# Windowed attention scores in blocks of 64 queries by 192 keys instead of strips of 32 by 160

## The chip, the cores and the metric

The program runs on one NeuronCore of a Trainium2 chip. The metric is the device time of one execution in microseconds (us). Three runs of the kernel before took 289.28, 289.46 and 292.43 us; the median is 289.46 us. The engines are PE (matrix multiply, with PEld for its weight loads), DVE (vector), ACT (scalar, does the exponentials), POOL and SP (issues most DMAs). PSUM is the memory that PE writes its results to, in banks of 512 fp32 per partition.

## The reference

Two parts are computed. The first is causal attention within a window of 128 keys, for 8 batches, 8 heads, 576 positions and a head size of 64, with a linear bias per head:

```python
scores = scale * np.matmul(q, k.transpose(0, 1, 3, 2))
rel = pos[:, None] - pos[None, :]
bias = slopes[:, None, None] * (-np.abs(rel))[None]
mask = (rel >= 0) & (rel < 128)
scores = np.where(mask, scores + bias[None], -1e9)
attn = softmax(scores); attn_out = attn @ v
```

The second is a soft mixture of experts over all 4608 tokens of 512 features: token logits against 32 slots, a softmax over the tokens that makes the slot inputs, two matrix products per expert (8 experts, 512 to 1024 to 512), and a softmax over the slots that mixes the slot outputs back.

## The kernel before, in words

**Groups.** The attention is done in 72 groups, one after another. A sequence of 576 queries is cut into four tiles of 128 queries (t = 0 to 3) and a tail of 64 (t = 4). A group is one tile and four heads (g = 0 or 1), or the tail with all eight heads: 9 groups per batch, 8 batches. In each group four slots of 128 by 128 scores are made, two per PSUM bank, and a pair of banks (`s4s`) alternates between even and odd groups. Heads of the two parities (par) lie in partitions 0 to 63 and 64 to 127, so a product over the 64 features of a head uses one half of the rows of the PE array, and the other parity the other half at the same time.

**Scores before.** For t of 1 to 4, the four strips of 32 queries go to four column ranges of the array (`64*32` in the rows: 64 array rows by 32 columns). Each strip sees its own 160 keys. L259 writes the bias as a product of ones with a ramp, eight matmuls of 320 columns in bf16; L266 adds q times k on top, sixteen matmuls of 160 columns in fp32, which the trace shows as 32 records, since an fp32 matmul is two. For t = 0 there is no earlier key: two bias matmuls of 256 columns (L247) and four score matmuls of 128 columns (L252, 8 records), all on `64*128` pieces of the array.

**The masked copy.** A query sees 128 keys, part of them in its own tile and part in the one before. `merge` folds the two onto 128 columns: `copy_predicated` overwrites one half with the other wherever a mask says so (L281, 512 columns for t of 1 to 3; L283, 256 columns for the tail). For t = 0, L279 writes a large negative number into the masked places instead.

**Order of the work.** All five engines' queues are written out by hand and run in order. Iteration i does, on DVE: `merge` of group i, row maximum (L301), reciprocal of the sums of group i-1 (L313), the exponent's bias (L304), normalising of group i-1 (L317). On ACT: the copy of the flipped probabilities of group i-3 (L379), now and then a copy of flipped attention outputs (L447) and of finished ones (L426), then four exponentials of group i (L357). POOL adds up for L313 (L309) and splits the flipped probabilities into the part for the own tile and the part for the one before (L381, L383). PE: transposes of group i-3 (L372), attention times v of group i-4 (L410), the scores of group i+1, then what the mixture needs (L438 transposes, L456 logits, L477 and L502 transposes, L514 slot sums). SP issues q, k, v and weight loads. After the 72 groups (from about 215 us) the experts and the mixing follow, which the diff does not touch.

Of the kernel before, what the change touches and what calls it, by code (L numbers as in the profile page):

```python
# [10 lines left out]
F32 = mybir.dt.float32  # L11
# [13 lines left out]
P = 128  # L25
# [9 lines left out]
KB = 32  # L35
# [21 lines left out]
def width(t):  # L57
    return P if t < 4 else TAIL

# [9 lines left out]
def tile_attn_softmoe(  # L69
# [20 lines left out]
    mask_u = cst[:, 0:P].bitcast(I32)  # L90
    mask_t = cst[:, P:P + TAIL].bitcast(I32)
# [14 lines left out]
    ramp = cpool.tile([P, 2, 2, WIN], BF16, name="ramp")  # L106
    ones = cpool.tile([P, P], BF16, name="ones")
    area = cpool.tile([P, 19, HW], F32, name="area")

    kall = kq[:, 0:NB * P].rearrange("p (n j w) -> p n j w", n=NB, j=NPAIR)  # L110
    qs = [kq[:, NB * P + 2 * P * i:NB * P + 2 * P * i + 2 * P] for i in range(3)]
# [66 lines left out]
    def load_k(b, t, eng=None):  # L178
        o, e = 4 * P * t, min(4 * P * (t + 1), NB * P)
        (eng or nc.sync).dma_start(kq[:, o:e], kd[b, :, o:e])  # L180
# [25 lines left out]
    with tc.manual_schedule(engines=ORDERED):  # L206
        warm = area[:, 2].bitcast(BF16)[:, 0:512]
        nc.vector.memset(warm, 0.0)
        nc.vector.memset(low, LOW)
        nc.vector.memset(ramp, 0.0)  # L210
        nc.vector.memset(ones, 1.0)
        nc.vector.memset(fine[:, 10:11], -1.0)
        nc.gpsimd.memset(cst[:, 0:P], 1.0)
# [12 lines left out]
        nc.gpsimd.memset(lgm, LOW)  # L226
        nc.gpsimd.memset(lne[:, :, NS:NS + 1], EPS)
        nc.gpsimd.memset(area[:, 3, 0:P], 1.0)
        nc.gpsimd.affine_select(
            unit_r, area[:, 3, 0:P], [[1, P]], ALU.is_equal, 0.0, base=0, channel_multiplier=-1)  # L230
        load_v()
        nc.scalar.dma_start(cst[:, P:], cstd)
        nc.scalar.dma_start(phi, phid)
        for t in range(2, NT):
            load_k(0, t)

    def scores(i):
        b, t, g = groups[i]
        s4 = s4s[i % 2]
        parts = [s4[:, 0:2], s4[:, 2:4]]  # L240
        if i == 0:
            parts = [ps_1.tile([P, 2, 2 * P], F32, tag="xp", name="s4_0"), pq[:, 0].rearrange("p (u w) -> p u w", u=2)]
            parts = parts[::-1]
        qt = qs[i % 3].rearrange("p (j w) -> p j w", w=width(t))
        if t == 0:
# [4 lines left out]
            for jj in range(2):  # L250
                for par, rows in enumerate(half):
                    nc.tensor.matmul(  # L252
                        parts[par][:, jj, 0:P], lhsT=qt[rows, jj], rhs=kall[rows, 0:4, 2 * g + jj],
                        start=False, stop=(jj == 1))
        else:
            strips = [(c // 2, c % 2) if t == 4 else (g, c) for c in range(4)]
            for par, rows in enumerate(half):
                for c, (h, r) in enumerate(strips):
# [3 lines left out]
            for jj in range(2):  # L262
                for par, rows in enumerate(half):
                    for c, (h, r) in enumerate(strips):
                        m0 = 4 * (t - 1) + r
                        nc.tensor.matmul(  # L266
                            s4[32 * c:32 * c + 32, 2 * par + jj, 32 * r:32 * r + WIN],
                            lhsT=qt[rows, 2 * h + jj if t == 4 else jj, 32 * r:32 * r + 32],
                            rhs=kall[rows, m0:m0 + 5, 2 * h + jj], start=False, stop=(jj == 1))
        st[groups[i]] = {"s4": s4, "parts": parts}  # L270

    ALL, LO, HI = slice(0, 4), slice(0, 2), slice(2, 4)

    def merge(key, us=ALL):
        t = key[1]
        s4 = st[key]["s4"]
        if t == 0:
            m = len(range(4)[us])
            nc.vector.copy_predicated(merged(key, us), bc(mask_u, 1, m), bc(low, 1, m).to_broadcast([P, m, P]))  # L279
        elif t < 4:  # L280
            nc.vector.copy_predicated(s4[:, :, P:2 * P], bc(mask_u, 1, 4), s4[:, :, 0:P])  # L281
        else:
            nc.vector.copy_predicated(s4[:, :, 0:TAIL], bc(mask_t, 1, 4), s4[:, :, P:P + TAIL])  # L283

    def merged_at(key):
        return P if 0 < key[1] < 4 else 0

    def merged(key, us):
        o = merged_at(key)
        if number[key] == 0:  # L290
            if isinstance(us, int):
                return st[key]["parts"][us // 2][:, us % 2, 0:P]
            return st[key]["parts"][us.start // 2][:, :, 0:P]
        return st[key]["s4"][:, us, o:o + P]

    def rowmax(key, us):
        if "mx" not in st[key]:
            o = P - merged_at(key)
            st[key]["mx"] = st[key]["s4"][:, :, o] if number[key] else work.tile([P, 4], F32, tag="mx", name="mx")
            st[key]["nb"] = work.tile([P, 4], F32, tag="nb", name="nb")  # L300
        nc.vector.tensor_reduce(st[key]["mx"][:, us], merged(key, us), axis=AX.X, op=ALU.max, negate=True)  # L301

    def bias(key, us):
        nc.vector.tensor_scalar_mul(st[key]["nb"][:, us], st[key]["mx"][:, us], SCALE)  # L304
# [46 lines left out]
    def expo(key, us=ALL):  # L351
        s = st[key]
        if "sm" not in s:
            s["p4"] = p4s[number[key] % 3]
            s["sm"] = work.tile([P, 4], F32, tag="sm", name="sm")
        for u in range(4)[us]:
            nc.scalar.activation(  # L357
                s["p4"][:, u], merged(key, u), AF.Exp,
                bias=s["nb"][:, u:u + 1], scale=SCALE, accum_out=s["sm"][:, u:u + 1],
            )  # L360

    def flip(key, us=ALL, to=None):
        s = st[key]
        if to is not None:
            s["pt"] = to.rearrange("p u (r w) -> p u r w", r=2)
            for u in range(4)[us]:
                nc.tensor.transpose(to[:, u], s["p4"][:, u], ident)
            return
        s["pt"] = pq_p.rearrange("p r (u w) -> p u r w", u=4)
        for u in range(4)[us]:  # L370
            for r, rows in enumerate(half):
                nc.tensor.transpose(s["pt"][:, u, r], s["p4"][rows, u], ident[rows, rows])  # L372

    def split(key, us=ALL):
        s, t = st[key], key[1]
        i = number[key] % 2 if number[key] < n - 1 else 2
        m = len(range(4)[us])
        pa, pp = pas[i], pps[i % 2]
        nc.scalar.copy(pa[:, us].rearrange("p u (r w) -> p u r w", r=2), s["pt"][:, us])  # L379
        if 0 < t < 4:  # L380
            nc.gpsimd.affine_select(  # L381
                pp[:, us], pa[:, us], [[0, m], [-1, P]], ALU.is_gt, 0.0, base=0, channel_multiplier=1)
            nc.gpsimd.affine_select(  # L383
                pa[:, us], pa[:, us], [[0, m], [1, P]], ALU.is_ge, 0.0, base=0, channel_multiplier=-1)
        elif t == 4:
            nc.gpsimd.affine_select(
                pp[:, us], pa[:, us], [[0, m], [0, 2], [-1, TAIL]], ALU.is_gt, 0.0, base=0, channel_multiplier=1)
            nc.gpsimd.affine_select(
                pa[:, us], pa[:, us], [[0, m], [0, 2], [1, TAIL]], ALU.is_ge, 0.0, base=0, channel_multiplier=-1)
        s.update(pd=pa, pp=pp)  # L390

    def values(key, pairs=None, to=None):
# [5 lines left out]
        pd, pp = st[key]["pd"], st[key]["pp"]  # L398
# [5 lines left out]
        for ph in parts:  # L404
            for i in inner:
                j = 2 * g + i
                for par in range(2):
# [4 lines left out]
                        rhs=src[:, 2 * par + i] if t < 4 else src[:, 2 * par + i % 2, TAIL * (i // 2):TAIL * (i // 2) + TAIL],  # L412
# [361 lines left out]
    with tc.manual_schedule(engines=ORDERED):  # L774
# [60 lines left out]
        split(gd, LO)  # L835
# [6 lines left out]
        split(gd, HI)  # L842
# [209 lines left out]
def constants():  # L1052
    slope = 2.0 ** (-8.0 * (np.arange(H, dtype=np.float64) + 1) / H)
    slopes = (slope.reshape(2, 2, 2, 1).transpose(2, 0, 1, 3) / SCALE * np.arange(WIN)).astype(BF16_NP)
    r = np.arange(P)
    cst = np.zeros((P, TAIL + NS), np.float32)
    cst[:, 0:TAIL] = np.arange(TAIL)[None, :] <= (r % TAIL)[:, None]
# [65 lines left out]
```

## Time and profile before

| | |
|---|---|
| three runs | 289.28, 289.46, 292.43 us |
| the profiled execution | 288.49 us, of which the span from the first to the last instruction is 286.0 us |
| PE busy in the span | 253.9 us (89%), 5535 matmul records |
| DVE busy | 221.6 us (77%) |
| ACT busy | 205.6 us (72%) |
| POOL busy | 112.9 us (39%) |
| DMA | 72.61 MB, mean 254 GB/s |

A busy time is a union: two records at once count once. The shares over the whole span mix two stages: the groups up to about 210 us, where PE, DVE and ACT are all busy most of the time, and the experts behind them, where PE alone works through. The chain of waits is followed back from the last instruction: each piece is the time by which it moved the end on, from the end of the piece before.

### The profile page before, as it was taken

The page shows a single profiled execution, that of the slowest core. Times are in us where ns is not written, and L with a number is a line of the kernel's source. Part 1 is how long each engine was busy: PE and PEld are TensorE (multiplying, and loading weights), DVE is VectorE, ACT ScalarE, POOL GpSimd, SP SyncE. Part 2 cuts the span into 40 slices and gives each one's busy share as a digit, 9 for nine tenths or more (in the row PEclk, how much of TensorE's full clock was granted, in tenths as well). Part 3 has the DMA queues.
Part 4 walks back from the last instruction along what each step waited for, and adds up shares of the span by engine and source line. Part 5 has one row for each costly group of instructions (what it writes and reads, how often), then busy time and mean ns, then how long its engine had stood idle before and what let it go on. Part 6 is the DMA issues. An engine that isn't in the chain of part 4 may idle for free.

```text
span 286.0 us, 13588 instructions
## 1 busy us (share of the span) xinstructions
PE 253.9 (89%) x5535; PEld 178.9 (63%) x5535; DVE 221.6 (77%) x509; ACT 205.6 (72%) x817; POOL 112.9 (39%) x218
## 2 busy tenths in 40 slices
PE   8588999799979889989979998998979899999990
PEld 4366676676757567667657765766756443687750
DVE  2889989998997999988998998798973352656451
ACT  2888889988888988998898988888783411044460
POOL 2044626662573276257527725466552011000000
PEclk9689999999999999999999999999999999999997
DMA  6645368869885987969797978866574579998997
GB/s 184 218 134 164 100 197 270 276 195 289 285 271 152 305 297 233 278 224 305 218 286 242 328 236 251 278 204 219 165 265 140 169 254 365 411 393 322 362 384 282
DMA packets 36754, 72.61 MB, mean 254 GB/s; under 512 B 4402, under 2 KB 15316, under 8 KB 36692
## 3 DMA queue, kind: packets, MB, share of 16 engines
q1 hardware_dynamic: 35972, 71.24, 75.7%
q8 instruction: 43, 0.70, 1.0%
q10 hardware_dynamic: 720, 0.51, 0.6%
q14 instruction: 19, 0.16, 0.2%
HBM read 62.29 MB, written 9.44 MB: 251 GB/s over the span
## 4 chain that ended last, share of the span: by engine, by line
PE 45%; DVE 23%; ACT 16%; POOL 7%; issue 5%; DMA 2%; DVEq 0%; ACTq 0%; POOLq 0%
ACT area L357 9%; PE xp L410 7%; DVE area L317 6%; DVE s L301 6%; PE s L266 5%; PE op L967 5%; PE hp L930 5%; PE po L992 4%; DVE s L281 3%; POOL area L381 3%; PE pq L372 3%; PE lp L456 2%; DVE s L279 2%; PE s L259 2%; ACT area L379 2%
## 5 line engine op out<-in xcount | busy, mean ns | idle before, releaser
L357 ACT ACTIVATE area<-s,nb 128x128 f32<-128x128 f32 x286 | 102.7, 391 | 13.8 <-DVE nb L304 10.4
L410 PE MATMUL xp<-area 128*64 128x128 f32 (+1 forms) x1104 | 74.5, 272 | 8.4 <-POOL area L381 5.3
L357 ACT ACTIVATION_READ_ACCUMULATOR area<-s,nb 128x1 f32 x286 | 65.4, 229 | 0.0
L410 PEld LDWEIGHTS xp<-area 128*64 128x64 f32 x1104 | 54.1, 137 | 18.0 <-POOL area L381 6.1
L317 DVE TENSOR_TENSOR area<-area,rs 128x512 f32<-128x512 f32 (+1 forms) x73 | 61.0, 836 | 1.6
L301 DVE TENSOR_REDUCE s<-s 128x4 f32<-128x512 f32 x71 | 49.5, 697 | 2.2
L379 ACT COPY area<-pq 128x512 f32<-128x512 f32 (+1 forms) x72 | 43.5, 605 | 10.7 <-PE pq L372 9.0
L266 PE MATMUL s<-kq 64*32 64x160 f32 x1792 | 43.8, 302 | 2.3 <-issue 2.3
L309 POOL TENSOR_SCALAR rs<-sm 128x4 f32<-128x4 f32 x70 | 15.0, 214 | 73.0 <-ACT area L357 71.6
L383 POOL TENSOR_SCALAR_AFFINE_SELECT area<-area 128x512 f32<-128x512 f32 x48 | 41.7, 870 | 3.3
L381 POOL TENSOR_SCALAR_AFFINE_SELECT area<-area 128x512 f32<-128x512 f32 x48 | 35.5, 740 | 15.5 <-ACT area L379 14.6
L281 DVE COPY_PREDICATED s<-cst,s 128x512 f32<-128x512 int32 x48 | 33.1, 689 | 6.1 <-PE s L266 5.6
L372 PE MATMUL pq<-unit_r,area 64*128 64x64 f32 x552 | 31.3, 233 | 3.7 <-ACT area L322 2.8
L266 PEld LDWEIGHTS s<-kq 64*32 64x32 f32 x1792 | 30.1, 107 | 4.1 <-issue 3.5
L372 PEld LDWEIGHTS pq<-unit_r,area 64*128 64x128 f32 x552 | 23.3, 140 | 11.8 <-issue 3.2
L259 PE MATMUL s<-ramp,ones 64*32 64x320 bf16 x448 | 18.7, 311 | 4.8 <-ACT area L357 4.5
L426 ACT COPY area<-xp 128x512 f32<-128x512 f32 (+1 forms) x37 | 21.4, 578 | 0.2
L447 ACT COPY area<-pq 128x512 f32<-128x512 f32 x34 | 20.7, 608 | 0.3 <-PE pq L432 0.3
L438 PEld LDWEIGHTS pq<-unit_r,area 64*128 64x128 f32 x264 | 11.1, 137 | 12.8 <-issue 9.7
L994 ACT COPY ob<-po 128x512 f32<-128x512 f32 x19 | 10.4, 591 | 11.4 <-PE po L992 11.4
L994 DVE COPY ob<-po 128x512 f32<-128x512 f32 x17 | 11.2, 686 | 6.6 <-PE po L992 6.5
L438 PE MATMUL pq<-unit_r,area 64*128 64x64 f32 x264 | 15.2, 233 | 0.9 <-ACT area L379 0.6
(173 smaller groups left out, 329.1 us busy)
## 6 DMA issues: line engine op xcount, KB each, us to landing
w<-w SPq DMA_DIRECT2D x53, 512.0 KB, 5.5
out<-ob SPq DMA_DIRECT2D x36, 256.0 KB, 3.9
kq<-q_t SPq DMA_DIRECT2D x69, 128.0 KB, 3.5
kq<-k_t SPq DMA_DIRECT2D x32, 256.0 KB, 3.9
area<-v_n SPq DMA_DIRECT2D x31, 256.0 KB, 4.2
area<-w SPq DMA_DIRECT2D x8, 512.0 KB, 4.6
area<-v_n SPq DMA_DIRECT2D x12, 128.0 KB, 4.4
kq<-w SPq DMA_DIRECT2D x3, 512.0 KB, 5.9
```

The lines of the kernel that those rows point to most:

```text
L259: nc.tensor.matmul(s4[32 * c:32 * c + 32, 2 * par:2 * par + 2, 32 * r:32 * r + WIN], lhsT=ones[rows, 0:32], rhs=ramp[rows, h], start=True, ...
L266: nc.tensor.matmul(s4[32 * c:32 * c + 32, 2 * par + jj, 32 * r:32 * r + WIN], lhsT=qt[rows, 2 * h + jj if t == 4 else jj, 32 * r:32 * r + 32],
L281: nc.vector.copy_predicated(s4[:, :, P:2 * P], bc(mask_u, 1, 4), s4[:, :, 0:P])
L301: nc.vector.tensor_reduce(st[key]["mx"][:, us], merged(key, us), axis=AX.X, op=ALU.max, negate=True)
L317: nc.vector.tensor_tensor(p4, p4, bc(rs, 2, P), op=ALU.mult)
L357: nc.scalar.activation(s["p4"][:, u], merged(key, u), AF.Exp, bias=s["nb"][:, u:u + 1], scale=SCALE, accum_out=s["sm"][:, u:u + 1],)
L372: nc.tensor.transpose(s["pt"][:, u, r], s["p4"][rows, u], ident[rows, rows])
L379: nc.scalar.copy(pa[:, us].rearrange("p u (r w) -> p u r w", r=2), s["pt"][:, us])
L381: nc.gpsimd.affine_select(pp[:, us], pa[:, us], [[0, m], [-1, P]], ALU.is_gt, 0.0, base=0, channel_multiplier=1)
L383: nc.gpsimd.affine_select(pa[:, us], pa[:, us], [[0, m], [1, P]], ALU.is_ge, 0.0, base=0, channel_multiplier=-1)
L410: nc.tensor.matmul(xp[D * par:D * par + D, j, 0:w], lhsT=v_slot[b, t - 1 + ph][:, D * h:D * h + D], rhs=src[:, 2 * par + i] if t < 4 else ...
L438: nc.tensor.transpose(xq[:, j, r], x[rows, j], ident[rows, rows])
```

## The change

`KB` goes from 32 to 64, so a block has 64 queries and a window of 128 + 64 = 192 keys. A slot no longer holds 128 queries of one head; it holds one half of the tile's queries (64) of two heads, the heads in the two partition halves. A PSUM bank then holds two slots with 2 x 192 columns.

- The bias of a bank is one matmul on a `64*128` piece with three rows that matter (two heads' ramps and, for t = 0, a row of large negative numbers), 384 columns in bf16; two matmuls per group replace eight (or the two of t = 0).
- The scores are eight matmuls on `64*64` pieces, 192 columns each (16 records), for t of 1 to 4; for t = 0 four of 64 and four of 128 columns.
- `merge` is one `copy_predicated` of 256 columns for every group, the first one in two halves.
- The layout of the slots changes in the row maximum, the transposes' destinations, POOL's patterns and the operand of attention times v; their counts and numbers of elements stay.
- The start has four small loads in place of two, and four POOL selects of 64 x 64 in place of one of 128 x 128.

On PE, the scores of a group with t > 0 and the two blocks behind them, the transposes of an earlier group and the products of a tail with v. Before (`s_0_83` is one of the two pairs of banks, `ones` the bias's weights, `pq` the transposes' bank, `xp` the bank of the products with v; of eight bias pairs the last is shown):

```order
L259 LDWEIGHTS ones
L259 MATMUL s_0_83<-ramp,ones 32x2x160
L266 MATMUL s_0_83<-kq 32x160 x16
L372 MATMUL pq<-unit_r,area 128x64 x8
L410 MATMUL xp<-area 64x64 x16
```

and with the change (the second of two bias pairs):

```order
L259 LDWEIGHTS pair_of
L259 MATMUL s_0_83<-ramp,pair_of 128x384
L267 MATMUL s_0_83<-kq 64x192 x8
L371 MATMUL pq<-unit_r,area 128x64 x8
L407 MATMUL xp<-area 64x64 x16
```

The order of the blocks is the same; the bias's product now spans all 128 columns of the array, and the scores' products, between it and the transposes, 64.

At a group with t = 0, on PE, before:

```order
L247 LDWEIGHTS ones
L247 MATMUL s_0_83<-ramp,ones 128x2x128
L247 LDWEIGHTS ones
L247 MATMUL s_0_83<-ramp,ones 128x2x128
L252 MATMUL s_0_83<-kq 128x128 x4
L372 MATMUL pq<-unit_r,area 128x64 x8
```

and with the change:

```order
L259 LDWEIGHTS pair_of
L259 MATMUL s_0_83<-ramp,pair_of 128x384
L267 MATMUL s_0_83<-kq 64x64 x4
L267 MATMUL s_0_83<-kq 64x128 x4
L371 MATMUL pq<-unit_r,area 128x64 x8
```

Here bias, scores and transposes all spanned 128 columns; now the scores between them span 64.

The diff, cut to its core:

```diff
-KB = 32
+KB = 64
...
+def slide(ap):
+    return bass.AP(ap.tensor, ap.offset, [list(ap.ap[0]), [KB, 2], [1, WIN]])
...
-        nc.gpsimd.affine_select(cst[:, 0:P], cst[:, 0:P], [[1, P]], ALU.is_gt, 0.0, base=0, channel_multiplier=-1)
+        nc.gpsimd.memset(mask, 1.0)
+        for c in range(2):
...
         for par in range(2):
-            nc.sync.dma_start(ramp[64 * par:64 * par + 1], slopes[par:par + 1])
+            nc.sync.dma_start(ramp[64 * par:64 * par + 3], slopes[par, :, 2 * P:])
+            nc.sync.dma_start(pair_of[64 * par:64 * par + 3], slopes[par, :, 0:2 * P])
...
-            for par, rows in enumerate(half):
-                nc.tensor.matmul(
-                    parts[par][:, :, 0:P], lhsT=ones[rows], rhs=ramp[rows, g, :, 0:P],
-                    start=True, stop=False)
...
-                    nc.tensor.matmul(
-                        s4[32 * c:32 * c + 32, 2 * par:2 * par + 2, 32 * r:32 * r + WIN],
-                        lhsT=ones[rows, 0:32], rhs=ramp[rows, h], start=True, stop=False)
...
-                            rhs=kall[rows, m0:m0 + 5, 2 * h + jj], start=False, stop=(jj == 1))
+        for par, rows in enumerate(half):
+            if t < 4:
+                dst, src = parts[par][:, 0:2 * WIN], slide(ramp[rows, g])
+            else:
+                dst, src = parts[par].rearrange("p (u w) -> p u w", u=2)[:, :, 0:WIN], ramp[rows, :, 0:WIN]
+            nc.tensor.matmul(dst, lhsT=pair_of[rows, int(t == 0)], rhs=src, start=True, stop=False)
+        for u in range(2):
+            h, hp = (u, g) if t < 4 else (0, u)
+            skip = max(2 * (1 - t) - h, 0)
+            m0 = 2 * (t - 1) + h
+            for par, rows in enumerate(half):
+                for jj in range(2):
+                    j = 2 * hp + jj
+                    nc.tensor.matmul(
+                        parts[par][KB * jj:KB * jj + KB, second * u + KB * skip:second * u + WIN],
+                        lhsT=qt[rows, jj if t < 4 else j, KB * h:KB * h + KB], rhs=kall[rows, m0 + skip:m0 + 3, j],
+                        start=False, stop=(u == 1))
...
-            nc.vector.copy_predicated(s4[:, :, P:2 * P], bc(mask_u, 1, 4), s4[:, :, 0:P])
...
+        x = ranges(key, us).rearrange("p a (x y) -> p a x y", y=KB)
+        m = x.shape[1]
+        if key[1] < 4:
+            to, of, keep = x[:, :, 0:6:5], x[:, :, 2:4], bc(mask.bitcast(I32), 1, m)
         else:
+            to, of, keep = x[:, :, 0:8:4], x[:, :, 2:8:4], bc(bc(mask[:, 0].bitcast(I32), 1, 2), 1, m)
+        nc.vector.copy_predicated(to, keep, of)
...
             nc.gpsimd.affine_select(
-                pp[:, us], pa[:, us], [[0, m], [-1, P]], ALU.is_gt, 0.0, base=0, channel_multiplier=1)
+                prev, own, [[-step, m], [0, 4], [-1, KB]], ALU.is_gt, 0.0, base=-i0, channel_multiplier=1)
...
-                        rhs=src[:, 2 * par + i] if t < 4 else src[:, 2 * par + i % 2, TAIL * (i // 2):TAIL * (i // 2) + TAIL],
+                        rhs=src[:, :, par, i] if t < 4 else src[:, i // 2, par, i % 2],
```

## Rows read from the trace of the kernel before

**Rows 1.** Busy time of each engine in stretches of the span: stretch, its length, then PE, PEld, DVE, ACT and POOL busy (records), granted clock, DMA share, GB/s.

```profile
8.00:16.00 8.00, 5.20 (x104) 3.63 (x104) 6.49 (x16) 6.29 (x29) 0.39 (x2) 0.58 0.65 207
...
150.00:170.00 20.00, 19.90 (x484) 15.02 (x486) 19.04 (x41) 18.00 (x78) 11.86 (x21) 1.00 0.87 278
...
16.00:209.00 193.00, 177.14 (x4462) 130.50 (x4448) 176.56 (x389) 171.08 (x717) 103.96 (x190) 1.00 0.75 236
```

**Rows 2.** The chain of waits in order of time, a stretch in which PE leads: start us, us by which the end moved on, what.

```profile
153.84 0.26 PE s L259 x8
154.10 0.54 PE s L266 x32
154.64 0.39 PE pq L372 x8
155.03 1.02 PE xp L410 x16
156.06 0.21 PE s L247 x2
156.27 0.45 PE s L252 x8
156.72 0.24 PE pq L438 x8
...
189.50 0.26 PE s L259 x8
189.76 0.54 PE s L266 x32
190.31 0.39 PE pq L438 x8
190.70 0.25 PE pq L372 x8
190.95 1.02 PE xp L410 x16
```

**Rows 3.** Groups of instructions by line, engine, operation and shape: count, busy us, mean ns of one, idle time before them and what ended it.

```profile
L281 DVE COPY_PREDICATED s<-cst,s 128x512 f32<-128x512 int32 x48 | 33.1, 689 | 6.1 <-PE s L266 5.6
...
L279 DVE COPY_PREDICATED s<-cst,fine 128x512 f32<-128x512 int32 x15 | 14.9, 997 | 0.1
...
L283 DVE COPY_PREDICATED s<-cst,s 128x256 f32<-128x256 int32 x8 | 3.4, 422 | 0.3 <-PE s L266 0.3
```

**Rows 4.** Who waited for whom between 16 and 205 us: us in total, times, longest.

```profile
PEld xp L410 <- POOL area L383: 5.4, 15, 0.6
PE xp L410 <- POOL area L381: 5.3, 6, 1.4
...
PE s L259 <- ACT area L357: 3.7, 8, 1.3
...
PE s L266 <- issue: 2.3, 4, 1.0
...
PE xp L410 <- POOL area L383: 1.3, 4, 0.4
...
PE xp L410 <- DMA area<-v_n: 0.9, 1, 0.9
```

**Rows 5.** The chain of waits in order of time, the pieces of the first scores behind the start and of the first and last masked copies on it.

```profile
11.80 0.47 PE s L259 x5
12.27 1.07 PE s L266 x24
...
15.01 0.40 PE s L259 x4
15.40 1.05 PE s L266 x25
...
16.48 0.71 DVE s L281
...
28.92 1.06 DVE s L279
...
31.99 0.62 DVE s L279
...
172.62 0.70 DVE s L281
...
205.92 1.06 DVE s L279
```

**Rows 6.** Instructions at the start in order of time: start us, us, engine (SPq is SP's DMA queue), line, operation, count, and in brackets the idle time before and what ended it.

```profile
1.56 0.59 SPq L218 DMA_DIRECT2D ramp<-slopes  x2
...
3.91 0.28 PEld L247 LDWEIGHTS <-ones 64*128 64x128 bf16 x2 [0.84 <-issue]
...
4.54 0.28 PEld L252 LDWEIGHTS pq<-kq 64*128 64x128 f32 x1 [0.34 <-DMA kq<-q_t]
```

**Rows 7.** POOL's split in two shapes by line: the pattern of 128-long runs (L383) and the tail's of 64-long runs (L388).

```profile
L383 POOL TENSOR_SCALAR_AFFINE_SELECT area<-area 128x512 f32<-128x512 f32 x48 | 41.7, 870 | 3.3
...
L388 POOL TENSOR_SCALAR_AFFINE_SELECT area<-area 128x512 f32<-128x512 f32 x7 | 5.3, 760 | 0.5
```

**Rows 8.** The chain of waits over the whole span, shares by engine, tile and line.

```profile
ACT area L357 9%; PE xp L410 7%; DVE area L317 6%; DVE s L301 6%; PE s L266 5%; PE op L967 5%; PE hp L930 5%; PE po L992 4%; DVE s L281 3%; POOL area L381 3%; PE pq L372 3%; PE lp L456 2%; DVE s L279 2%; PE s L259 2%; ACT area L379 2%
```

More of the change, by code (lines that the diff above doesn't have):

```diff
@@ L105, in tile_attn_softmoe @@
     kq = cpool.tile([P, 3 * UW], F32, name="kq")
-    ramp = cpool.tile([P, 2, 2, WIN], BF16, name="ramp")
-    ones = cpool.tile([P, P], BF16, name="ones")
+    ramp = cpool.tile([P, 2, 2 * P], BF16, name="ramp")
+    pair_of = cpool.tile([P, 2, P], BF16, name="pair_of")
     area = cpool.tile([P, 19, HW], F32, name="area")
-    kall = kq[:, 0:NB * P].rearrange("p (n j w) -> p n j w", n=NB, j=NPAIR)
-    qs = [kq[:, NB * P + 2 * P * i:NB * P + 2 * P * i + 2 * P] for i in range(3)]
+    kall = kq[:, 0:NPAIR * S].rearrange("p (n j w) -> p n j w", n=NB, j=NPAIR)
+    qs = [kq[:, NPAIR * S + 2 * P * i:NPAIR * S + 2 * P * i + 2 * P] for i in range(3)]
     half = [slice(64 * par, 64 * par + 64) for par in range(2)]
@@ L210, in tile_attn_softmoe @@
         nc.vector.memset(ramp, 0.0)
[L211 removed]
+        nc.vector.memset(pair_of, 0.0)
         nc.vector.memset(fine[:, 10:11], -1.0)
[L213 to L214 removed]
+        nc.gpsimd.memset(mask, 1.0)
+        for c in range(2):
+            rows = slice(KB * c, KB * c + KB)
+            nc.gpsimd.affine_select(
+                mask[rows, 0], mask[rows, 0], [[-1, KB]], ALU.is_ge, 0.0, base=0, channel_multiplier=1)
+            nc.gpsimd.affine_select(
+                mask[rows, 1], mask[rows, 1], [[1, KB]], ALU.is_gt, 0.0, base=0, channel_multiplier=-1)
         load_k(0, 0)
@@ L238, in scores @@
         b, t, g = groups[i]
[L239 to L240 removed]
         if i == 0:
[L242 to L243 removed]
+            parts = [pq[:, 0], ps_1.tile([P, 4 * P], F32, tag="xp", name="s4_0")]
+        else:
+            parts = [s4s[i % 2][:, 2 * par:2 * par + 2].rearrange("p u w -> p (u w)") for par in range(2)]
         qt = qs[i % 3].rearrange("p (j w) -> p j w", w=width(t))
[L245 to L269 removed]
@@ L285, in merged_at @@
-    def merged_at(key):
-        return P if 0 < key[1] < 4 else 0
-    def merged(key, us):
[L289 to L294, printed above, removed]
+        second = WIN if t < 4 else 2 * P
+        for par, rows in enumerate(half):
+            if t < 4:
+                dst, src = parts[par][:, 0:2 * WIN], slide(ramp[rows, g])
+            else:
+                dst, src = parts[par].rearrange("p (u w) -> p u w", u=2)[:, :, 0:WIN], ramp[rows, :, 0:WIN]
+            nc.tensor.matmul(dst, lhsT=pair_of[rows, int(t == 0)], rhs=src, start=True, stop=False)
@@ L296, in rowmax, with ranges @@
+    def ranges(key, us):
+        if number[key] == 0:
+            return st[key]["parts"][us.start // 2].unsqueeze(1)
+        return st[key]["s4"]
+    def merged(key, us):
+        return ranges(key, us).rearrange("p a (u w) -> p a u w", u=2)[:, :, :, 0:P]
     def rowmax(key, us):
-        if "mx" not in st[key]:
-            o = P - merged_at(key)
-            st[key]["mx"] = st[key]["s4"][:, :, o] if number[key] else work.tile([P, 4], F32, tag="mx", name="mx")
+        if "nb" not in st[key]:
@@ L371, in flip @@
             for r, rows in enumerate(half):
-                nc.tensor.transpose(s["pt"][:, u, r], s["p4"][rows, u], ident[rows, rows])
+                nc.tensor.transpose(s["pt"][:, 2 * (u % 2) + u // 2, r], s["p4"][rows, u], ident[rows, rows])
     def split(key, us=ALL):
-        s, t = st[key], key[1]
+        s, (b, t, g) = st[key], key
         i = number[key] % 2 if number[key] < n - 1 else 2
-        m = len(range(4)[us])
         pa, pp = pas[i], pps[i % 2]
         nc.scalar.copy(pa[:, us].rearrange("p u (r w) -> p u r w", r=2), s["pt"][:, us])
-        if 0 < t < 4:
+        if t:
+            own, prev = (
+                x[:, us].rearrange("p u w -> p (u w)").rearrange("p (h x w) -> p h x w", x=4, w=KB) for x in (pa, pp))
+            m, step = own.shape[1], KB if t < 4 else 0
+            i0 = step * (us.start // 2)
             nc.gpsimd.affine_select(
-                pp[:, us], pa[:, us], [[0, m], [-1, P]], ALU.is_gt, 0.0, base=0, channel_multiplier=1)
+                prev, own, [[-step, m], [0, 4], [-1, KB]], ALU.is_gt, 0.0, base=-i0, channel_multiplier=1)
             nc.gpsimd.affine_select(
[L384 to L389, printed above, removed]
+                own, own, [[step, m], [0, 4], [1, KB]], ALU.is_ge, 0.0, base=i0, channel_multiplier=-1)
         s.update(pd=pa, pp=pp)
@@ L397, in values @@
         xp = st[b, t]
-        pd, pp = st[key]["pd"], st[key]["pp"]
+        pd, pp = (st[key][x].rearrange("p (h a) (j w) -> p h a j w", a=2, j=2) for x in ("pd", "pp"))
         parts = (1,) if t == 0 else (0, 1)
@@ L834, in tile_attn_softmoe @@
         flip(gd, LO, bank("pt"))
-        split(gd, LO)
+        split(gd, EVEN)
         total(gd, HI)
@@ L841, in tile_attn_softmoe @@
         flip(gd, HI, quarters(free[2]))
-        split(gd, HI)
+        split(gd, ODD)
         token_sum(end)
@@ L1053, in constants @@
     slope = 2.0 ** (-8.0 * (np.arange(H, dtype=np.float64) + 1) / H)
-    slopes = (slope.reshape(2, 2, 2, 1).transpose(2, 0, 1, 3) / SCALE * np.arange(WIN)).astype(BF16_NP)
+    ramp = np.zeros((2, 3, 2, 2 * P))
+    ramp[:, 0:2] = slope.reshape(2, 2, 2, 1).transpose(2, 1, 0, 3) / SCALE * np.arange(2 * P)
+    ramp[:, 2, :, 0:P] = LOW
+    pair_of = np.zeros((2, 3, 2, P))
+    for jj in range(2):
+        pair_of[:, jj, :, KB * jj:KB * jj + KB] = 1.0
+    pair_of[:, 2, 1] = 1.0
+    slopes = np.concatenate([pair_of.reshape(2, 3, 2 * P), ramp.reshape(2, 3, 4 * P)], axis=2).astype(BF16_NP)
     r = np.arange(P)
     cst = np.zeros((P, TAIL + NS), np.float32)
-    cst[:, 0:TAIL] = np.arange(TAIL)[None, :] <= (r % TAIL)[:, None]
     cst[:, TAIL:] = np.arange(NS)[None, :] == (r % NS)[:, None]
```

32 lines of the change are left out of this document (14 added, 18 removed).

## The prediction, made before the changed kernel had run

> **What bounds the kernel now.** I read the busy times by stretch first, then the chain of waits, then the groups by shape, then the waits. Before the experts there are 72 groups in a row, and the stretch from 16 to 209 us holds 67 of them (2.88 us each). There the reader sees three engines side by side: PE 177.1 of 193.0 us, DVE 176.6, ACT 171.1 [rows 1]. No one engine is the bound throughout, but in the 20 us from 150 on PE has 19.90 us [rows 1], and the chain there is one PE block behind another [rows 2]. So what PE gets on top counts nearly in full in such stretches, and what DVE saves there counts for nothing.
>
> **The change part by part.** The masked copy: 48 copies of 512 columns at 689 ns and 15 with the large number at 997 ns become copies of 256 columns, for which the tail's copies give 422 ns [rows 3]. That is 48 x 0.27 + 15 x 0.575 = 21.4 us of DVE, 0.3 us per group: DVE goes from 176.6 to some 156 us in the stretch. The other DVE, ACT and POOL instructions keep their counts and sizes; POOL's new pattern has runs of 64, and the tail's row with such runs is no slower than the one with runs of 128 (760 against 870 ns) [rows 7]. I cost these at nothing; POOL is idle nearly half of the time, so a tenth more there would stay hidden.
>
> The bias on PE: eight matmuls of 320 columns moved the chain on by 0.26 us, the two of 256 columns (t = 0) by 0.21 us [rows 2]. Two of 384 columns lie between 0.26 and 0.31 us; I take 0.28.
>
> The scores on PE: for t = 0, eight records of 128 columns, two at a time, take 0.45 us, so a turn of 128 columns takes 0.11 us. Before, 32 records of 160 columns, eight at a time, take 0.54 us, four turns of 0.135 us [rows 2]. The time goes by columns and turns, not by the number of records. The new block has 16 records of 192 columns on four pieces of the array: four turns of 0.16 to 0.17 us, 0.66 us together. For t = 0 it is two turns of 64 and two of 128 columns: 0.33 us.
>
> The seam between bias and scores: before, both ran on pieces of the same shape (64 x 32, or 64 x 128 for t = 0), and the scores cost only their turns. Now the bias runs on 64 x 128 pieces and the scores on 64 x 64. What a change of the piece costs can be read: the transposes (64 x 128) behind the scores of t = 0 (also 64 x 128) add 0.24 us, behind the scores of the other groups (64 x 32) 0.39 us, and 0.25 us behind other transposes [rows 2]. So 0.14 us goes by when the column width changes although the rows of the array stay split in the same way. No row has 64 x 128 followed by 64 x 64; its bounds are 0 (the next block's start would hide it) and 0.17 us (products with v behind transposes: 1.02 us for eight turns of 0.107). I take 0.14, the row of the same kind of change. The Trainium skill ("TensorEngine Tiling (Array Packing)", Key Properties) says that a change of tiling mode, as against another tile of the same mode, drains the engine; by it the new seam costs like the others, and without it one might take 0 for a seam where only columns change. The 0.24 and 0.39 us of this trace agree with it.
>
> Sum per group with t > 0: 0.28 + 0.66 + 0.14 = 1.08 us in place of 0.26 + 0.54 = 0.80, so 0.28 more. For t = 0: 0.28 + 0.33 + 0.14 = 0.75 in place of 0.66, and the transposes behind them now also stand at a seam, 0.14 more: 0.23. In the stretch that is 54 x 0.28 + 13 x 0.23 = 18.1 us, and PE's busy time becomes 195.2 us, more than the whole stretch lasts now. PE becomes the bound everywhere.
>
> How long the stretch then gets depends on how many of PE's waits go. Not given back are the stalls that no engine causes (2.3 us in the scores' products, "issue") and the wait for v (0.9 us) [rows 4]: 195.2 + 3.2 = 198.4 us. In the other direction, some waiting is counted as busy: the weight loads for the products with v waited 5.4 us for POOL's second select where the matmuls show only 1.3 us of idle time [rows 4], so up to 4.1 us of the 195.2 can vanish. Bounds: 194.3 us (+1.3) if every wait on POOL, ACT and DVE goes, 211.1 us (+18.1) if all stay. I take 197 us, **+4.0**: the nearest row is the stretch from 150 us, where PE led and its visible waits were 0.1 us in 20 [rows 1], and of the hidden ones I give back a third.
>
> The rest: two score blocks behind the start run at a granted clock of 0.58 on the mean [rows 1] and took 0.47 + 1.07 and 0.40 + 1.05 us, all on the chain [rows 5]; by 1.08/0.80 they grow by 1.05 us. On SP's queue two more small loads go ahead of the second part of k. Two such issues took 0.59 us; the first bias stood at 3.91 us, but the first scores waited until 4.54 us for q [rows 6], so most of it is hidden: between 0 and 0.6 us, I take 0.2. The last masked copy of 1.06 us on the chain, at 205.9 us [rows 5], falls to 0.42, and PE is less full there: -0.6. Behind 209 us nothing changes. Sum: 4.0 + 1.05 + 0.2 - 0.6 = +4.65 us on the profiled execution's 288.49, 293.1 us. The median of the three runs, 289.46, is 0.97 above that execution, so **294 us**.
>
> **The rivals.**
> *The seam costs nothing, and DVE's relief carries (20%).* Then a group costs PE 0.14 us more for t > 0 and about nothing for t = 0: 7.6 us in the stretch, 184.7 us busy, below 193. For it: nothing in the trace has this very seam, and the masked copies stand on the chain with 3% (L281) and 2% (L279) of the span, 8.6 and 5.7 us, the scores' products with 5%, 14.3 us [rows 8]. Replaced along that chain, the copies give 8.6 x 0.39 + 5.7 x 0.58 = 6.6 us, and the products take 14.3 x 0.12/0.54 = 3.2 back: at most -3.4. Since ACT at 171 us and PE follow closely, I expect two thirds of it, -2.2 us, 287.3 us. It decides if the seam is under some 0.05 us, so that PE with its stalls stays at about 190 us. Against it: 0.39 against 0.24 us.
> *PE's waits stay (10%).* If POOL's splits and ACT's exponentials release PE as late as now (5.3 and 3.7 us [rows 4]), since they in turn follow PE's transposes, the 18.1 us come on top with little absorbed: +10 to +18 us, 300 to 307 us. Against it: the stretch from 150 us.
> *Fewer instructions pay (4%).* 40 records per group become 18. If each cost time of its own, PE would gain and DVE's relief would show: with ACT's 171 us as the next bound I put 282 us. Against it: 40 records in 0.80 us are 20 ns each, and they are explained by columns alone. The Trainium skill ("TensorEngine Tiling (Array Packing)", Instruction Overhead) gives some 60 cycles of overhead per matmul; by that, 22 matmuls fewer, at 2.4 GHz, would be an estimated 0.55 us per group. The trace disagrees, since 0.55 us is already two thirds of the whole 0.80.
> *The four 64 x 64 pieces don't all run at once (3%).* With two at a time the scores take 1.32 us, +44 us in the stretch, about 335 us. Against it: pieces split by rows and pieces split by columns both overlap here.
>
> **How the numbers follow.** The forecast, PE as the bound with the seam paid, gets 63%, with a range of its own from 290.5 (the lower bound) to 298.5 us. Something over 1%, 2.9 us, is what a measurement of this kernel can tell from no change: below 286.6 or above 292.4 us. Faster: 8 of the 20 points of the first rival and the 4 of the third, 12%. Within 1%: the other 12 and some 23 of the forecast's 63, 35%. Slower: 40 + 10 + 3 = 53%. The range from 286.5 to 300 leaves out about 8 points of the first rival, 4 of the third, 5 of the second and the fourth's 3.
>
> **What would show it.** In the profile after: PE busy 97% or more of the stretch and the stretch 196 to 199 us long; the seam as an end-to-end piece of 0.8 us for the 16 score records where 0.66 would be its absence; the masked copy at 422 ns; DVE falling to some 80% busy and ACT to 87%; PE's waits on POOL gone. If the piece for the scores is 0.66 us, the first rival holds; if PE waits on POOL and ACT as before, the second. The prediction is wrong if PE's busy time is not the stretch's bound, that is, if it lies below some 188 us.

## The result and the profile after

The changed kernel took 290.31 us (median of 12 runs, 289.56 to 291.12) against 289.79 us of the kernel before in the same session; the ratio is 1.0064, 95% interval [1.0039, 1.0089], some 1.9 us slower. The ratio compares fast runs alone, while the 289.79 us is a median over slower runs of the kernel before as well, so the two medians differ by 0.5 us only. In a later session, in the last experiment below, the ratio was 1.0021 [0.9984, 1.0058]. The forecast was 294 us, 1.6% slower: the time lies in the wide range of 286.5 to 300 us, a little under the 290.5 us at which the forecast's own range began, and the step is two fifths of the one forecast, or less.

The profiled execution took 290.67 us and has a span of 288.9 us. The chain of waits, shares by engine: first the kernel before, then the kernel after, and of the latter also the shares by line (L267 are the scores' products, L259 the bias, L407 the products with v, L371 and L435 the transposes):

```profile
PE 45%; DVE 23%; ACT 16%; POOL 7%; issue 5%; DMA 2%; DVEq 0%; ACTq 0%; POOLq 0%
...
PE 72%; ACT 9%; DVE 7%; POOL 5%; DMA 3%; issue 2%; DVEq 0%; ACTq 0%; SPq 0%
PE xp L407 16%; PE s L267 14%; PE pq L371 6%; PE op L964 5%; PE s L259 5%; PE hp L927 5%; ACT area L356 4%; PE po L989 3%; PE pq L435 3%; PE ap L511 3%; PE lp L453 2%; POOL area L383 2%; DVE area L314 2%; DVE s L297 2%; DMA area<-v_n 2%
```

PE has gone from 45% of the chain to 72%; the masked copies, 5% before [rows 8], are no longer in the list. The pieces of the kernel after in order of time, start us, us by which the end moved on, one group with t > 0, one with t = 0:

```profile
155.57 0.27 PE s L259 x2
155.83 0.81 PE s L267 x16
156.65 0.39 PE pq L371 x8
157.04 1.02 PE xp L407 x16
158.06 0.27 PE s L259 x2
158.33 0.50 PE s L267 x16
158.83 0.39 PE pq L435 x8
```

Against [rows 2]: bias and scores 1.08 us where 0.80 stood; for t = 0 bias, scores and the transposes behind them 1.16 us where 0.90 stood. The other blocks are as long as before. Busy time by stretch (columns as in [rows 1]):

```profile
8.00:16.00 8.00, 6.42 (x62) 3.63 (x60) 5.85 (x18) 6.16 (x29) 0.39 (x2) 1.00 0.59 195
...
16.00:209.00 193.00, 188.31 (x3358) 129.22 (x3356) 158.07 (x386) 169.86 (x714) 102.29 (x187) 1.00 0.75 236
```

In the long stretch PE rose by 11.2 us, DVE fell by 18.5, ACT hardly moved. Who waited for whom, 16 to 205 us (columns as in [rows 4]): two rows of the kernel before, then the kernel after:

```profile
ACT area L379 <- PE pq L372: 8.7, 14, 1.3
...
DVE s L281 <- PE s L266: 5.2, 7, 1.4
```

```profile
ACT area L377 <- PE pq L371: 15.0, 19, 1.6
DVE s L283 <- PE s L267: 12.9, 26, 1.4
...
PEld xp L407 <- POOL area L385: 2.6, 9, 0.3
...
PE xp L407 <- POOL area L383: 1.6, 4, 0.4
...
PE s L259 <- ACT area L356: 1.3, 2, 1.0
...
PE xp L407 <- DMA area<-v_n: 0.7, 1, 0.7
```

PE's waits on POOL and ACT shrank to about a third (5.3 to 1.6, 3.7 to 1.3 us), the weight loads' wait for POOL's second select to a half (5.4 to 2.6 us [rows 4]), and the 2.3 us without a cause inside the scores' products are gone. In their place DVE and ACT wait for PE more than before (5.2 to 12.9, 8.7 to 15.0 us). Where the time of the span came from is read off the row maxima, one per group: the fourth group's, the fifth's and the last but one's. First the kernel before, then the one after, then a second execution of the one after (experiment 8), each in order of time:

```profile
14.19 0.70 DVE L301 TENSOR_REDUCE s<-s 128x4 f32<-128x512 f32 x1
...
17.21 0.70 DVE L301 TENSOR_REDUCE s<-s 128x4 f32<-128x512 f32 x1
...
207.00 0.70 DVE L301 TENSOR_REDUCE s<-s 128x4 f32<-128x512 f32 x1
```

```profile
14.92 0.70 DVE L297 TENSOR_REDUCE s<-s 128x4 f32<-128x512 f32 x1
...
18.17 0.70 DVE L297 TENSOR_REDUCE s<-s 128x4 f32<-128x512 f32 x1
...
208.59 0.70 DVE L297 TENSOR_REDUCE s<-s 128x4 f32<-128x512 f32 x1
```

```profile
14.68 0.70 DVE L297 TENSOR_REDUCE s<-s 128x4 f32<-128x512 f32 x1
...
209.18 0.70 DVE L297 TENSOR_REDUCE s<-s 128x4 f32<-128x512 f32 x1
```

The start cost 0.73 us, and the 67 groups between took 193.67 in place of 192.81 us: 0.86 us more, though PE does about 0.27 us more in each, 18 us in all. The second execution needed 194.50 us for them, 1.69 us more, so this figure is good to about a microsecond. Behind the groups the first execution lost about another 1.3 us (the second 0.8), 0.48 of them in a stall without a shown cause, at 254.65 us among the experts' products, which the diff does not touch. Busy time in just these 67 groups (columns as in [rows 1]), before, after and the second execution:

```profile
14.19:207.00 192.81, 177.02 (x4460) 130.04 (x4458) 176.13 (x388) 170.30 (x716) 102.51 (x188) 1.00 0.76 237
```

```profile
14.92:208.59 193.67, 188.98 (x3358) 129.71 (x3356) 158.74 (x389) 170.13 (x713) 102.14 (x187) 1.00 0.75 235
```

```profile
14.68:209.18 194.50, 189.68 (x3358) 130.10 (x3356) 159.50 (x389) 170.04 (x713) 102.03 (x187) 1.00 0.75 234
```

PE's busy time rose by 12.0 us (12.7 in the second execution), and its idle time fell from 15.8 to 4.7 us (4.8).

### The profile page after: what moved, and what is told of

Same layout as the page of the kernel before. It is cut to its first block, busy times and chain, and to the rows that moved or that the text cites. A ratio compares the mean times of both kernels' runs of the same rounds, so it can differ in the third digit from the quotient of the medians.

```text
span 288.9 us, 11388 instructions
## 1 busy us (share of the span) xinstructions
PE 268.8 (93%) x4431; PEld 178.6 (62%) x4431; DVE 203.1 (70%) x509; ACT 205.7 (71%) x817; POOL 113.1 (39%) x221
## 4 chain that ended last, share of the span: by engine, by line
PE 72%; ACT 9%; DVE 7%; POOL 5%; DMA 3%; issue 2%; DVEq 0%; ACTq 0%; SPq 0%
PE xp L407 16%; PE s L267 14%; PE pq L371 6%; PE op L964 5%; PE s L259 5%; PE hp L927 5%; ACT area L356 4%; PE po L989 3%; PE pq L435 3%; PE ap L511 3%; PE lp L453 2%; POOL area L383 2%; DVE area L314 2%; DVE s L297 2%; DMA area<-v_n 2%
## 5 line engine op out<-in xcount | busy, mean ns | idle before, releaser
L407 PE MATMUL xp<-area 128*64 128x128 f32 (+1 forms) x1104 | 73.0, 271 | 2.9 <-POOL area L383 1.6
L267 PE MATMUL s<-kq 64*64 64x192 f32 (+2 forms) x1144 | 60.7, 328 | 0.0
L407 PEld LDWEIGHTS xp<-area 128*64 128x64 f32 x1104 | 53.8, 137 | 11.1 <-POOL area L385 2.6
L383 POOL TENSOR_SCALAR_AFFINE_SELECT area<-area 128x512 f32<-128x512 f32 (+1 forms) x57 | 44.3, 777 | 28.0 <-ACT area L377 26.5
L297 DVE TENSOR_REDUCE s<-s 128x4 f32<-128x512 f32 (+1 forms) x72 | 50.0, 694 | 2.2
L385 POOL TENSOR_SCALAR_AFFINE_SELECT area<-area 128x512 f32<-128x512 f32 (+1 forms) x57 | 46.3, 812 | 3.9
L267 PEld LDWEIGHTS s<-kq 64*64 64x64 f32 x1144 | 35.1, 137 | 14.3 <-issue 12.2
L283 DVE COPY_PREDICATED s<-cst,s 128x256 f32<-128x256 int32 (+1 forms) x72 | 30.4, 422 | 14.6 <-PE s L267 14.1
L371 PE MATMUL pq<-unit_r,area 64*128 64x64 f32 x552 | 31.5, 233 | 1.2 <-ACT area L319 0.8
L371 PEld LDWEIGHTS pq<-unit_r,area 64*128 64x128 f32 x552 | 23.1, 140 | 10.7 <-issue 3.3
L259 PE MATMUL s<-ramp,pair_of 64*128 64x384 bf16 x143 | 25.0, 342 | 2.1 <-ACT area L356 2.1
L310 DVE RECIPROCAL rs<-rs 128x4 f32<-128x4 f32 (+1 forms) x73 | 12.5, 172 | 9.8 <-POOL rs L306 9.2
L435 PEld LDWEIGHTS pq<-unit_r,area 64*128 64x128 f32 x264 | 10.7, 137 | 13.7 <-issue 11.9
L259 PEld LDWEIGHTS <-pair_of 64*128 64x128 bf16 x144 | 7.6, 93 | 16.2 <-issue 9.3
```

Of the source, the lines that this page charges most:

```text
L259: nc.tensor.matmul(dst, lhsT=pair_of[rows, int(t == 0)], rhs=src, start=True, stop=False)
L267: nc.tensor.matmul(parts[par][KB * jj:KB * jj + KB, second * u + KB * skip:second * u + WIN], lhsT=qt[rows, jj if t < 4 else j, KB * h:KB ...
L283: nc.vector.copy_predicated(to, keep, of)
L297: nc.vector.tensor_reduce(st[key]["mx"], merged(key, us), axis=AX.X, op=ALU.max, negate=True)
L371: nc.tensor.transpose(s["pt"][:, 2 * (u % 2) + u // 2, r], s["p4"][rows, u], ident[rows, rows])
L383: nc.gpsimd.affine_select(prev, own, [[-step, m], [0, 4], [-1, KB]], ALU.is_gt, 0.0, base=-i0, channel_multiplier=1)
```

## The experiments

Four kernels shared a chip and its runs of the kernel before (288.74 us), and four more another (289.82 us). Ratios are to the kernel before of the same session. The changed kernel itself ran beside experiments 5 to 7 only, so 1 to 4 are compared with it through ratios of different sessions.

**1. The seam taken out.** The bias of a bank in two halves of 64 columns, so that it runs on the same pieces as the scores:

```diff
-            nc.tensor.matmul(dst, lhsT=pair_of[rows, int(t == 0)], rhs=src, start=True, stop=False)
+            for jj in range(2):
+                cols = slice(KB * jj, KB * jj + KB)
+                nc.tensor.matmul(dst[cols], lhsT=pair_of[rows, int(t == 0), cols], rhs=src, start=True, stop=False)
```

> The bias of a bank is written by two matmuls on 64 x 64 pieces in place of one on a 64 x 128 piece, so bias and scores run on pieces of one shape; nothing else changes. Theory (PE is the bound of the changed kernel, and 0.14 us per group go at the seam between bias and scores): the score block's piece of the chain falls from 0.81 to about 0.66 us, PE's busy time in the groups' stretch falls by about 9 us, and, since ACT and DVE come close behind, 5 to 8 us of that reach the end: 282 to 285 us, faster than the kernel before. Rival 1 (the 0.14 us is the latency of the scores themselves and has nothing to do with the shape): the piece stays at 0.81, time within 1 us of 290.3. Rival 2 (the seam goes, but waits on POOL and ACT take its place): the piece falls to 0.66, time within 2 us of 290.3.

Measured: 284.03 us, ratio 0.9823 [0.977, 0.9876]. The chain's pieces of this kernel (L261 bias, L269 scores), a group with t > 0 and one with t = 0:

```profile
83.80 0.29 PE s L261 x4
84.08 0.65 PE s L269 x16
84.73 0.39 PE pq L437 x8
...
104.42 0.29 PE s L261 x4
104.71 0.33 PE s L269 x16
105.04 0.39 PE pq L437 x8
```

The scores' piece falls from 0.81 to 0.65 us, and the bias, with twice the matmuls, costs 0.29 in place of 0.27. So the change of the piece's width between bias and scores costs 0.16 us, and 72 groups less 0.14 us each, 10 us of PE, brought some 6 to 7 us at the end (2.0 and 2.4 points under the changed kernel's two ratios), in the theory's range. Rivals 1 and 2 fall. The chain of the whole span is now this:

```profile
PE 49%; ACT 24%; DVE 10%; POOL 8%; issue 4%; DMA 2%; DVEq 0%; ACTq 0%; SPq 0%; POOLq 0%
```

PE is back near the 45% of before, and ACT follows. The term of the expectation that missed is the busy time: PE still shows 185.15 us in the stretch from 16 to 209 us, not 9 us less, because the stretch now holds more of the program; between the same two row maxima (14.23 and 203.30 us here) it is 181.8 us, 7.2 less than in the changed kernel.

**2. DVE's saving given back to the changed kernel:**

```diff
         nc.vector.copy_predicated(to, keep, of)
+        if key[1] < 4:
+            for _ in range(1 if key[1] else 2):
+                nc.vector.copy_predicated(to[:, :, 0:1], keep[:, :, 0:1], of[:, :, 0:1])
```

> The changed kernel with the masked copy's saving given back to VectorE: one more copy of 128 columns per group (two for t = 0) that writes the same values again, about 0.29 us each, 23 us of DVE in all, a little over the 21 us that the change took off. Theory (PE is the bound, DVE at 158 of 193 us has slack): DVE rises to about 179 us, the time by 1 to 4 us, 291 to 294 us. Rival (DVE's relief is what held the loss at 0.6%, that is, PE's added time was paid for by DVE's): 8 us or more, 298 us and up.

Measured: 293.85 us, ratio 1.0176 [1.0128, 1.0225], 1.1 points over the changed kernel's 1.0064 and 1.6 over its 1.0021, 3 to 4.5 us. The rows by shape show what was given back, 23.0 us:

```profile
L283 DVE COPY_PREDICATED s<-cst,s 128x256 f32<-128x256 int32 x71 | 30.0, 423 | 6.5 <-PE s L267 6.3
L286 DVE COPY_PREDICATED s<-cst,s 128x128 f32<-128x128 int32 x78 | 23.0, 295 | 2.7
```

That is in the theory's range, and the rival is out. Without DVE's relief the change would have cost 1.8%. About four fifths of the 23 us are absorbed: PE is the bound of the changed kernel, but DVE at 158 of 193 us is not far enough off to be free, and its relief is worth something. In the 67 groups, between this kernel's row maxima (columns as in [rows 1]), PE is idle for 7.0 us where the changed kernel had 4.7:

```profile
16.12:212.01 195.89, 188.92 (x3372) 129.66 (x3368) 176.72 (x461) 170.49 (x715) 102.66 (x188) 1.00 0.73 233
```

**3. DVE's saving alone, on the kernel before:**

```diff
-            nc.vector.copy_predicated(merged(key, us), bc(mask_u, 1, m), bc(low, 1, m).to_broadcast([P, m, P]))
+            nc.vector.copy_predicated(
+                merged(key, us)[:, :, 0:64], bc(mask_u[:, 0:64], 1, m), bc(low, 1, m).to_broadcast([P, m, 64]))
...
-            nc.vector.copy_predicated(s4[:, :, P:2 * P], bc(mask_u, 1, 4), s4[:, :, 0:P])
+            nc.vector.copy_predicated(s4[:, :, P:P + 64], bc(mask_u[:, 0:64], 1, 4), s4[:, :, 0:64])
```

> The kernel before with the masked copies of t = 0 to 3 cut to 64 of the 128 columns of each slot (256 in all); this leaves out half of the masking. It is the change's relief of DVE alone, about 19 to 21 us, without any change on PE. Theory (three engines side by side, ACT at 171 and PE with its true blocks at about 172 us follow at once): 2 to 5 us faster, 285 to 288 us. Rival (DVE bounded the kernel before): 8 us or more faster, 282 us and less. Rival 2 (DVE's relief is worth nothing): within 1 us.

Measured: 285.2 us, ratio 0.9883 [0.9829, 0.9937], 3.4 us faster, in the theory's range. Less was taken off DVE than written, as the rows by shape show:

```profile
L282 DVE COPY_PREDICATED s<-cst,s 128x256 f32<-128x256 int32 x48 | 20.3, 423 | 7.0 <-PE s L266 6.5
L279 DVE COPY_PREDICATED s<-cst,fine 128x256 f32<-128x256 int32 x15 | 11.8, 788 | 0.1
```

The 48 copies halve as expected, but those that write the large number still take 788 ns, not 422. So DVE lost 15.9 us (33.1 + 14.9 [rows 3] less 20.3 + 11.8), and a fifth of it reached the end. DVE alone did not bound the kernel before.

**4. Two loads at the start in place of four,** on top of experiment 1; ramp and weights of the bias lie in one tile:

```diff
-            nc.sync.dma_start(ramp[64 * par:64 * par + 3], slopes[par, :, 2 * P:])
-            nc.sync.dma_start(pair_of[64 * par:64 * par + 3], slopes[par, :, 0:2 * P])
+            nc.sync.dma_start(lines[64 * par:64 * par + 3], slopes[par])
```

> The first run's kernel, with ramp and weights of the bias in one tile, so that two small loads at the start take the place of four. Theory (the first groups start 0.7 us late since the last of four loads lands at 4.7 us): the first bias matmul starts at about 4.2 us in place of 4.8, and the time is 0.3 to 0.7 us under the first run's. Rival (the start is hidden behind the first wait for v or for the clock): no difference to the first run, within 0.2 us.

Measured: 282.61 us, ratio 0.9799 [0.9751, 0.9847]. The first bias matmul starts at 4.45 us, where experiment 1's stood at 4.66 and the changed kernel's at 4.83 (4.59 in its second execution). In order of time, first experiment 1, then this kernel, the first bias matmuls and a later block of them:

```profile
4.66 0.53 PE L261 MATMUL pq<-ramp,pair_of 64*64 64x384 bf16 x2 [0.68 <-DMA pair_of<-slopes]
...
5.87 0.72 PE L261 MATMUL s<-ramp,pair_of 64*64 64x384 bf16 x4
```

```profile
4.45 0.46 PE L260 MATMUL pq<-lines 64*64 64x384 bf16 x2 [0.47 <-DMA lines<-slopes]
...
5.12 0.40 PE L260 MATMUL s<-lines 64*64 64x384 bf16 x4
```

The load is still what it waits for, and it came 0.2 us earlier, not the 0.6 us expected. The same block of four takes 0.40 us in this execution and 0.72 in that of experiment 1, and why is not shown. The interval overlaps that of experiment 1, so this kernel's own gain, some 0.7 us by the ratios, is not certain, nor that the loads made it. This kernel is faster than both the kernel before (by 2.0%) and the changed one.

**5. PE's added load alone, on the kernel before:**

```diff
             strips = [(c // 2, c % 2) if t == 4 else (g, c) for c in range(4)]
+            for par, rows in enumerate(half):
+                nc.tensor.matmul(
+                    parts[par][:, :, 0:WIN], lhsT=ones[rows], rhs=ramp[rows, g], start=True, stop=True)
```

> The kernel before with PE's added load alone: ahead of the eight bias matmuls of each group with t > 0 stand two more of 320 columns on 64 x 128 pieces, whose result the bias writes over, so that a group costs PE about 0.27 us more, 15 us in all; DVE keeps its full masked copies. Theory (some 5 to 7 us of what counts as busy PE before is waiting inside the blocks, besides 10 us of visible waits, and both are used up first): 4 to 8 us slower than before, and the piece of the products with v on the chain stays 1.02 us. Rival (PE's busy time is all work, as the prediction mostly took it): 10 us or more slower.

Measured: 294.65 us, ratio 1.0163 [1.0098, 1.0229], 4.7 us slower. The chain's pieces of this kernel (L258 the two added matmuls, L262 the eight of the bias):

```profile
159.16 0.24 PE s L258 x2
159.40 0.26 PE s L262 x8
159.66 0.54 PE s L269 x32
```

The added block costs 0.24 us in 56 groups, 13.4 us, and 4.7 us come out, so two thirds of PE's added work did not show in the time, although DVE kept its full copies. In the 67 groups PE's idle time fell from 15.8 to 10.5 us, which is 5.3 us of it; that the rest went into waiting that counts as busy is argued, not shown. The rival falls. The prediction's own sum misses this kernel on the other side: 177.1 + 13.4 + 3.2 - 1.4 = 192.3 us, no longer than the stretch before, because it lets every visible wait on another engine go. Here two thirds of PE's idle time stay.

**6. Both loads at once, without the change's layout** (the edits of 3 and 5 together):

> The kernel before with both loads of the change and none of its layout: masked copies cut to 256 columns (half of the masking of t = 0 to 3 is left out) and the two added bias matmuls per group with t > 0. Theory (the change is the sum of PE's 0.27 us per group and DVE's 0.3 us, nothing else): within 0.6% of the changed kernel's ratio, 0 to 3 us slower than before. Rival 1 (the prediction's size, since waits are not given back): 4.5 us or more slower. Rival 2 (the smaller number of instructions, 18 records in place of 40 per group, helped the changed kernel by itself): 3 us or more slower than the changed kernel.

Measured: 291.24 us, ratio 1.0087 [1.0052, 1.0121], 2.5 us slower than before: by 0.2 and 0.7 points above the changed kernel's two ratios. The second is a little more than the theory allowed; this kernel's DVE relief is some 4 us smaller, for the reason in 3, and its t = 0 groups are not burdened. Rival 1 falls, and by the time so does rival 2 at its price of 3 us. But the agreement in time is in part chance. Busy time of this kernel in the 67 groups, between its row maxima (columns as in [rows 1]):

```profile
13.11:209.72 196.61, 186.44 (x4561) 133.55 (x4560) 164.88 (x388) 170.73 (x715) 99.34 (x187) 1.00 0.75 233
```

Its start is 1.6 to 1.8 us shorter than the changed kernel's, and its 67 groups take 196.61 us, 2.1 to 2.9 us longer, with 10.2 us of idle PE in place of 4.7. So in the groups the two loads alone do not make up the changed kernel; that fewer instructions, or something else of the new layout, are worth some 2 us there is not excluded.

**7. No seam, but DVE's saving given back** (the edits of 1 and 2):

> The first run's kernel (bias and scores on pieces of one shape) with VectorE's saving given back as in the second run. Theory (without the seam PE and DVE are side by side again, so DVE's relief is worth as much there as in the kernel before, 3 to 5 us): 3 to 6 us slower than the first run, within 0.7% of the kernel before. Rival (with the seam gone nothing is bound by DVE): within 1.5 us of the first run.

Measured: 291.19 us, ratio 1.0075 [1.0043, 1.0107], 2.5 points above experiment 1 (of the other session), some 7 us: more than the 3 to 6 us expected, and the rival is out. With PE less full, the same 23 us on DVE cost about twice as much as in experiment 2.

**8. The changed kernel again,** next to experiments 5 to 7:

> The changed kernel once more, on the same chip as these runs. Theory: 1 to 3 us slower than before, 6 to 8 us slower than without the seam. Rival (the 0.6% was a matter of the chip): no difference to before.

Measured: 290.17 us, ratio 1.0021 [0.9984, 1.0058]. That is 0.6 us, under the 1 to 3 us expected, and alone this run could not tell it from no change, so it does not rule out the rival. With the first result the change costs 0.2 to 0.6%. Experiment 1's ratio lies 2.0 points below this one, 5.7 us, a little under the 6 to 8 us expected, and 2.4 points below the first result's.

## Why the prediction was wrong

**Right, to a few hundredths.** The masked copy of 256 columns (forecast 422 ns, measured 424). The bias of 384 columns (0.28; 0.27). The scores by turns and columns plus the seam (0.66 + 0.14 = 0.80; 0.81, and 0.65 without the seam). For t = 0 0.23 us more per group; 0.26. The seam's price was taken from transposes behind scores, another pair of shapes, and held; the Trainium skill's rule that a change of tiling mode drains the engine ("TensorEngine Tiling (Array Packing)", Key Properties) agrees with the 0.16 us of experiment 1. That PE becomes the bound: it has 72% of the chain, and taking 0.14 us per group off it gave 6 to 7 us.

**Wrong: the step from PE's added work to the length of the stretch.** The prediction added 18.1 us to a busy time of 177.1 us, kept 3.2 us of stalls, and gave back a third of the 4.1 us that it had found hidden in the busy time: +4.0 us. Measured on the row maxima it is +0.86 us, and +1.69 in the second execution. The added work was there in full, block by block, but PE's busy time in the same 67 groups rose by 12.0 us only (12.7). About 0.8 of the missing 6 us are other blocks that fall outside the two row maxima, by their counts and pieces; the other 4.6 to 5.3 us are, by this balance, waiting that had counted as busy. That is the term that was mis-sized: the prediction gave back 1.4 us of such waiting. Where it stood is not shown in full, since of the weight loads' 5.4 us only 2.8 are seen to go. The term for idle time erred the other way: 4.7 us were left where 3.2 had been kept, and they are other waits than those named, since the 2.3 us of stalls did not come back. The text named the end of the range that was nearly right, 194.3 us with every wait given back, and then chose the middle.

That so many waits could go is in part DVE's relief, which the prediction held to count for nothing where PE leads: without it PE is idle for 2.3 us more (experiment 2). It is not all of it, since experiment 6, with most of the relief, leaves 10.2 us idle. Experiment 5 adds 13.4 us of work without it, and 4.7 us come out; experiment 3 gives the relief alone, -3.4 us; experiment 2 takes it away again, 3 to 4.5 us. The sum of 5 and 3, +1.3 us, lies between the changed kernel's two results, but both together measured 2.5 us (experiment 6), and in the groups they are 2 to 3 us apart from the changed kernel, so this split is rough. It is luck, too, that the total came as near as it did: the 0.8 to 1.3 us lost behind the groups stand in no term of the forecast.

**The small terms.** The start cost 0.73 us at the fourth group, which has the first of the two slow score blocks before it, and 0.96 us at the fifth, behind both, where 0.2 + 1.05 was forecast. The two blocks grew by 0.46 and 0.17 us on the chain (their lines are in the last section, those before in [rows 5]), 0.63 us in all, and the late loads made the other 0.33 us. In the second execution the fifth group was 1.06 us late. The relief at 205.9 us (-0.6) did not come; the last groups were bound by PE as well.

**The rivals.** "The seam costs nothing" falls by the 0.81 us, "PE's waits stay" by the waits after, and four pieces at once do overlap: four turns of 0.16 us. "Fewer instructions pay" falls at its price of 282 us; a smaller gain, some 2 us in the groups, is not excluded (experiment 6). The Trainium skill ("TensorEngine Tiling (Array Packing)", Instruction Overhead) gives each matmul an overhead of some 60 cycles, and counted for every matmul that would have them pay; in experiment 1 twice the bias matmuls cost 0.02 us.

What stays open is why PE's stalls without a cause vanished. The four kernels with the layout of before (experiments 3, 5 and 6 among them) show 1.7 to 3.5 us of them in the groups, the six with the new layout none. Experiment 6, 16 to 209 us:

```profile
PE s L269 <- issue: 1.1, 3, 0.7
...
PE xp L414 <- issue: 0.8, 1, 0.8
...
PE pq L376 <- issue: 0.4, 1, 0.4
```

The profile's queue of instruction loads (q8) moved 0.57 MB with the change in place of 0.70, so the number of instructions may be behind it, but it differs together with the rest of the layout, and no run separates the two.

## What to carry to other kernels

When an engine that shares the bound gets more work, first fill its waits, and price them from the pieces of the chain (block by block, end to end) and not from a busy time, in which short waits are hidden: work added to one of three nearly full engines came out at a third (experiment 5), work taken off at a fifth (experiment 3). Once it leads nearly everywhere, a microsecond counts about two thirds (experiment 1). And what another engine saves is not free of value then, since some of these waits are on that engine (3 to 4.5 us in experiment 2). Where two blocks of matmuls with different shapes of array pieces follow each other in every round, try to give them one shape, even with twice the number of matmuls: that turned a loss of 0.6% into a gain of 1.8%.

## What the runs showed that was not expected

The granted clock in the profile of the changed kernel is 1.00 from 8 to 16 us, as the first of the two stretches above shows (0.58 before [rows 1]), but the same kind of block there takes nearly twice its later time. This kernel, in order of the chain:

```profile
12.40 0.51 PE s L259 x2
12.90 1.49 PE s L267 x16
...
16.06 0.43 PE s L259 x2
16.50 1.19 PE s L267 x16
```

against 0.27 and 0.81 us later. Its first two pieces take 1.8 to 1.9 times as long as later. In the kernel before the same blocks took 1.8 to 2.0 times as long (0.47 to 0.26 and 1.07 to 0.54 us [rows 2, 5]) at a recorded clock of 0.58 on the mean. So the durations speak for the lower of the two levels, 1.2 in place of 2.4 GHz, which the clock's record does not show here; that is an inference, and no run settles it. And a masked copy that takes its data as one number per partition, spread over 256 columns, took 788 ns on the mean where one with data from PSUM took 423 ns (experiment 3); by halving the columns only a fifth of its 997 ns went.
